# One-core gated mix of linear attention and dilated local attention: resident weight stages, crossbar-transposed x, overlapping key tiles with row-tiled scores, Wo folded into KV

## The chip, the cores and the metric

The kernel runs on one core of a Trainium2 chip. Its time is the device time of one execution in microseconds (us). Engine names are those of the profile: PE is TensorE's matmul, PEld its weight load, DVE is VectorE, ACT is ScalarE, POOL is GpSimd, SP is SyncE, which issues the DMAs.

Ratios are the mean time of one kernel's runs over the mean of the kernel before in the same rounds on the same chip, so they are not quite the ratio of the medians quoted beside them. Where two edited kernels are compared, I take the difference of their ratios times 620 us and say so.

## The reference

The sequence has S = 2048 rows, D = 1024 columns and H = 32 heads of width 32. Both halves read the same `x`.

```python
g = sigmoid((x * gate_w).sum(-1))
# A: linear attention, H = 32 heads of width 32
q, k, v = heads(x @ A_wqkv);  pq, pk = phi(q), phi(k)     # phi(t) = max(t,0) + min(exp(t),1) + 1e-6
kv = einsum("sd,se->de", pk, v);  z = pk.sum(s)           # per head
a = ((pq @ kv) / (pq @ z + 1e-6)) @ A_wo
# B: each query sees 8 keys: its own row, 2, 4, ... 14 rows earlier
q, k, v = heads(x @ B_wqkv)
b = (softmax(q . k[s - 2w], w = 0..7) @ v) @ B_wo
out = g * a + (1 - g) * b                                  # [1, 2048, 1024], bf16
```

## The kernel before

It works in four blocks of 512 rows. Each block loads its rows of `x`, computes the gate from them, transposes them on TensorE, projects, and does B's attention for 8 groups of four heads (a "head group" is 128 columns). A's queries and B's results go to DRAM. When KV is complete, an output phase reads them back, one tile of 128 rows after another.

```python
for t in range(4):                                   # per block: load, gate, transpose
    eng.dma_start(out=xtile[:], in_=x[tb * 128:(tb + 1) * 128, :])
    nc.vector.tensor_tensor_reduce(out=gjunk[:], in0=xtile[:], in1=gw_row[:], ..., accum_out=gdot[:])
    ...
    for kt in range(KT):
        nc.tensor.transpose(out=xps[:, kt, :], in_=xtile[:, kt * 128:(kt + 1) * 128], identity=ident[:])
    # evacuated into xT by VectorE or ScalarE
...
for c in range(KT):                                  # B: per head group; k, q and A's q are projected (cut)
    for i in range(4):                               # queries masked to one head each
        nc.vector.tensor_scalar(out=qm[:, :, i, :], in0=uq_v, scalar1=headmask4[:, i:i + 1], ...)
    for t in range(4):                               # 128 queries against this and the previous 128 keys
        nc.tensor.matmul(s2[:, 0, :], lhsT=kT512[:, c, qcols], rhs=qm_flat, start=True, stop=True)
        nc.tensor.matmul(s2[:, 1, :], lhsT=prev_keys, rhs=qm_flat, start=True, stop=True)
        # exp (ScalarE), mask (VectorE), then per head two PV matmuls of 33 columns, reciprocal, scale, transpose
    nc.sync.dma_start(out=OBT_d[b4, :, c, :], in_=OBTpiece[:])
...
# output phase, per 128 rows: numA and denA from KVbd and Zbd, scale to OA, 8 transposes to OAT,
# then 32 matmuls with the two Wo, copied out and stored
```

The softmax here doesn't subtract the row's maximum and nothing guards it: scores larger than these inputs give would overflow.

## Time and profile before

The time is 620.0 us (median of 4 runs, 619.11 to 620.95).

| What | before |
|---|---|
| PE busy / share of the span | 581.7 us / 94% |
| DVE busy | 355.9 us (58%) |
| ACT busy | 278.9 us (45%) |
| PE's share of the chain that ended last | 84% |
| PE issue time summed from the timeline (estimate) | 557 us of a span of 618.1 us |

Three parts of the page: the first line of busy times, and two rows of the 40 slices (tenths of each slice busy, and the clock granted to TensorE in tenths).

```profile
PE 581.7 (94%) x3980; PEld 284.8 (46%) x4056; DVE 355.9 (58%) x1165; ACT 278.9 (45%) x489; POOL 5.3 (1%) x22
...
PE   3999999979999998999999989999997999999997
...
PEclk9999999999999999999999989999999899999999
```

PE is almost always busy, so a change has to take work away from PE, or close its few gaps. A matmul's recorded duration (about 380 ns for 512 columns) overlaps its neighbour's; the pace has to be read from the chain or the timeline. The first line below is from the chain (start, length, what), the others from PE's timeline of one head group.

```profile
32.53 10.74 PE pj L187 x49
```

```profile
201.07 0.18 PE L301 MATMUL oB<-Vaug,PT 128*128 128x33 bf16 x1
201.10 0.18 PE L303 MATMUL oB<-Vaug,PT 128*128 128x33 bf16 x1
201.12 0.18 PE L301 MATMUL oB<-Vaug,PT 128*128 128x33 bf16 x1
```

A 512-column matmul costs about 0.215 us of issue (the 10.74 us hold 49 of them and the rest of the last one's duration), and a 33-column one 0.025 us, whatever its recorded 0.18 us says. With these paces 2048 projection and output matmuls take 440 us, 248 score matmuls 53 us, 992 PV matmuls 25 us, 384 transposes 21 us, the rest 17 us. The other 60 us are gaps. The view of windows shows the largest: the start, the joints between blocks, and the joint to the output phase. PE is idle for 26 us in these five rows; the rest lies elsewhere or is covered by recorded durations and was not located (columns: length, then busy time and count of each engine, then clock, DMA share and GB/s).

```profile
0.00:14.20 14.20, 3.67 (x32) 3.44 (x33) 9.77 (x48) 3.00 (x6) 5.29 (x22) 1.00 0.86 298
122.00:145.00 23.00, 19.32 (x133) 9.76 (x135) 19.33 (x61) 11.15 (x20) 0.00 (x0) 1.00 0.30 87
236.00:264.00 28.00, 24.04 (x175) 12.06 (x175) 23.57 (x75) 13.07 (x23) 0.00 (x0) 1.00 0.18 53
353.00:380.00 27.00, 24.13 (x160) 11.82 (x162) 18.73 (x55) 11.67 (x18) 0.00 (x0) 0.94 0.05 16
466.00:487.00 21.00, 16.01 (x152) 9.20 (x153) 16.30 (x56) 9.58 (x19) 0.00 (x0) 0.84 0.49 114
```

### The profile page before, as it was taken

To read this page: it belongs to the slowest core of one execution; us is meant where nothing else is said; L and a number is where in the kernel's file an instruction comes from. 1 tells how busy PE (TensorE), PEld (TensorE's weight loads), DVE (VectorE), ACT (ScalarE), POOL (GpSimd) and SP (SyncE) were. 2 spreads that over 40 slices of the span, in tenths; PEclk is the share of its full clock that TensorE was granted. 3 is DMA by queue.
4 is the path that set the end of the run, shared out by engine and by line. 5 is a ranking of instruction groups with operands and counts; after the bars stand their busy time and mean duration, and the time that the engine had idled before them with its cause. 6 is when DMAs were issued, how large, how long until landed. Compare 5 with 4: busy or idle time off the path is not lost.

```text
span 618.1 us, 10399 instructions
## 1 busy us (share of the span) xinstructions
PE 581.7 (94%) x3980; PEld 284.8 (46%) x4056; DVE 355.9 (58%) x1165; ACT 278.9 (45%) x489; POOL 5.3 (1%) x22
## 2 busy tenths in 40 slices
PE   3999999979999998999999989999997999999997
PEld 2445444444444444345444444454443555445443
DVE  6523788892048889801788873058888533444441
ACT  2333666643347666333666643346666122122111
POOL 3000000000000000000000000000000000000000
PEclk9999999999999999999999989999999899999999
DMA  8970001040001003000000100062013333444311
GB/s 305 398 265 1 27 26 35 32 122 2 0 10 35 27 27 103 10 0 1 27 27 27 35 28 0 1 223 81 30 36 101 83 79 89 103 103 103 85 52 35
DMA packets 57666, 42.88 MB, mean 69 GB/s; under 512 B 35984, under 2 KB 48272, under 8 KB 57616
## 3 DMA queue, kind: packets, MB, share of 16 engines
q1 hardware_dynamic: 57616, 42.22, 21.7%
q8 instruction: 31, 0.51, 0.3%
q14 instruction: 19, 0.16, 0.1%
HBM read 29.62 MB, written 12.58 MB: 68 GB/s over the span
## 4 chain that ended last, share of the span: by engine, by line
PE 84%; DVE 7%; ACT 3%; DMA 2%; issue 2%; SPq 0%; ACTq 0%
PE pj L187 22%; PE po L373 18%; PE pjk L240 9%; PE pjq L245 9%; PE pja L257 8%; DVE pk L195 2%; PE oB L303 2%; PE oB L301 2%; PE tr L316 2%; PE numA L349 1%; DMA xtile<-in_A_x_dram 1%; PE kvp L218 1%; ACT e L192 1%; DVE e L193 1%; DVE qm L252 1%
## 5 line engine op out<-in xcount | busy, mean ns | idle before, releaser
L187 PE MATMUL pj<-WAkv,xT 128*128 128x512 bf16 x500 | 116.7, 385 | 7.6 <-DVE pk L195 3.4
L187 PEld LDWEIGHTS <-xT 128*128 128x128 bf16 x768 | 74.9, 98 | 99.4 <-issue 15.1
L240 PE MATMUL pjk<-xT,WBqk 128*128 128x512 bf16 x251 | 73.7, 379 | 0.6
L257 PE MATMUL pja<-xT,WAq 128*128 128x512 bf16 x246 | 63.3, 378 | 0.6
L245 PE MATMUL pjq<-xT,WBqk 128*128 128x512 bf16 x245 | 62.9, 378 | 0.7
L373 PE MATMUL po<-Wo_sb,OAT 128*128 128x512 bf16 x241 | 61.9, 382 | 1.1
L373 PE MATMUL po<-Wo_sb,obtblk 128*128 128x512 bf16 x239 | 61.2, 379 | 0.1
L220 DVE TENSOR_TENSOR KVacc<-KVacc,kvp 128x129 f32<-128x129 f32 x32 | 8.3, 289 | 87.2 <-PE kvp L218 87.2
L187 PE MATMUL pj<-WBv,xT 128*128 128x512 bf16 x250 | 55.4, 379 | 0.3
L252 DVE TENSOR_SCALAR qm<-uq,headmask_118 128x512 bf16<-128x512 bf16 x128 | 42.1, 346 | 15.7 <-ACT uq L248 15.7
L378 DVE CAST osb<-po 128x512 bf16<-128x512 f32 x16 | 11.1, 692 | 54.9 <-ACT osb L376 54.9
L301 PE MATMUL oB<-Vaug,PT 128*128 128x33 bf16 x480 | 40.2, 179 | 0.0
L303 PE MATMUL oB<-Vaug,PT 128*128 128x33 bf16 x480 | 39.5, 178 | 0.0
L313 DVE TENSOR_TENSOR Obc<-oB,scb 128x128 bf16<-128x128 f32 x128 | 36.7, 287 | 1.5
L301 PEld LDWEIGHTS <-PT 128*128 128x128 bf16 x480 | 33.0, 97 | 9.4 <-DVE PT L293 7.7
L260 ACT ACTIVATE ea<-pja 128x512 f32<-128x512 f32 x32 | 19.1, 597 | 37.6 <-PE pja L257 37.4
L198 ACT CAST vA<-pj 128x512 bf16<-128x512 f32 x32 | 18.8, 588 | 37.6 <-PE pj L187 37.6
L192 ACT ACTIVATE e<-pj 128x512 f32<-128x512 f32 x32 | 19.1, 597 | 36.2 <-PE pj L187 32.6
L309 DVE RECIPROCAL scb<-oB 128x4 f32<-128x4 f32 x128 | 23.0, 179 | 21.4 <-PE oB L303 20.6
L240 PEld LDWEIGHTS <-WBqk 128*128 128x128 bf16 x256 | 24.4, 97 | 23.5
L202 ACT CAST Vaug<-pj 128x512 bf16<-128x512 f32 x32 | 18.8, 588 | 36.0 <-PE pj L187 33.8
L245 PEld LDWEIGHTS <-WBqk 128*128 128x128 bf16 x256 | 22.8, 97 | 23.7
(825 smaller groups left out, 901.9 us busy)
## 6 DMA issues: line engine op xcount, KB each, us to landing
xtile<-in_A_x_dram SPq DMA_DIRECT2D x16, 256.0 KB, 4.5
WAkv<-in_A_wqkv_dram SPq DMA_DIRECT2D x16, 256.0 KB, 5.4
WBqk<-in_B_wqkv_dram SPq DMA_DIRECT2D x8, 512.0 KB, 8.1
pqT_d<-pqpiece SPq DMA_DIRECT2D x32, 128.0 KB, 1.9
OBT_d<-OBTpiece SPq DMA_DIRECT2D x32, 128.0 KB, 1.9
out_dram<-osb SPq DMA_DIRECT2D x32, 128.0 KB, 2.6
pqblk<-pqT_d SPq DMA_DIRECT2D x15, 256.0 KB, 3.5
obtblk<-OBT_d SPq DMA_DIRECT2D x15, 256.0 KB, 3.1
```

The lines of the kernel that those rows point to most:

```text
L187: nc.tensor.matmul(pj[:], lhsT=xT[:, kt, xcols], rhs=Wsrc[:, kt, col0:col0 + 512], start=(kt == 0), stop=(kt == KT - 1))
L192: nc.scalar.activation(out=e[:], in_=pj[:], func=ACT.Exp)
L240: nc.tensor.matmul(pjk[:], lhsT=WBqk[:, kt, wcols_k], rhs=xT[:, kt, :], start=(kt == 0), stop=(kt == KT - 1))
L245: nc.tensor.matmul(pjq[:], lhsT=WBqk[:, kt, wcols_q], rhs=xT[:, kt, :], start=(kt == 0), stop=(kt == KT - 1))
L252: nc.vector.tensor_scalar(out=qm[:, :, i, :], in0=uq_v, scalar1=headmask4[:, i:i + 1], scalar2=None, op0=ALU.mult)
L257: nc.tensor.matmul(pja[:], lhsT=WAq[:, kt, wcols_q], rhs=xT[:, kt, :], start=(kt == 0), stop=(kt == KT - 1))
L260: nc.scalar.activation(out=ea[:], in_=pja[:], func=ACT.Exp)
L301: nc.tensor.matmul(oB[:, i, :], lhsT=PT[:, 1, i, :], rhs=Vaug_prev[:, h, :], start=True, stop=False)
L303: nc.tensor.matmul(oB[:, i, :], lhsT=PT[:, 0, i, :], rhs=Vaug_cur[:, h, :], start=False, stop=True)
L309: nc.vector.reciprocal(out=scb[:], in_=oB[:, :, Dh:Dh + 1])
L313: nc.vector.tensor_tensor(out=Obc[:], in0=oB[:, :, 0:Dh], in1=scb[:].broadcast_to([P, 4, Dh]), op=ALU.mult)
L373: nc.tensor.matmul(po[:, nch, :], lhsT=lhsT, rhs=Wo_sb[:, c16, nch * 512:(nch + 1) * 512], start=(c16 == 0), stop=(c16 == 2 * KT - 1))
```

## The change

The intent is to reorganise the kernel into three stages over all 2048 rows, with everything resident on the chip:

1. All of `x` is loaded transposed by the DMA crossbar. A's keys and values, then KV. A's `Wo` is folded into KV (`W2 = KV @ Wo` per head group), so that A's output needs one matmul in place of numerator, transpose and output; the scaling moves to the queries.
2. B: 18 query tiles of 113 rows (the first has 127), each against its own 128 keys that overlap the neighbour's by 15, so that one key tile suffices. Values are projected for each of the 18 tiles. Scores use 32-row tiles of the array, the four heads of a group in four row groups.
3. A's queries, denominators by a matmul with a block of ones times z, `1/den` as exp(-ln(den)), then both outputs; the gate is applied at evacuation.

The new code, cut to its core:

```diff
+    nc.sync.dma_start_transpose(out=xT[:, :, 0:128], in_=x[0:128, :])
+    WkA = load_w("WkA", A_wqkv, D)
+    for s0, s1_ in ((128, 512), (512, 1024), (1024, S)):
+        nc.sync.dma_start_transpose(out=xT[:, :, s0:s1_], in_=x[s0:s1_, :])
...
-                xps = ps_pj.tile([P, KT, P], BF16, name="xps", tag="pj")
-                for kt in range(KT):
-                    nc.tensor.transpose(out=xps[:, kt, :], in_=xtile[:, kt * 128:(kt + 1) * 128],
-                                        identity=ident[:])
...
+            trk = ps_kv.tile([P, P], BF16, name="trk", tag="kv")
+            nc.tensor.transpose(out=trk[:], in_=kvm[:], identity=ident[:])
+            nc.scalar.copy(out=KVT[:, c, :], in_=trk[:])
...
+                nc.tensor.matmul(w2p[:], lhsT=KVT[:, c, :], rhs=WoA[half][:, c, :],
+                                 start=True, stop=True)
...
+                for q0, w, k0 in tiles:                  # three tiles per group
+                    for i in range(4):
+                        r = slice(32 * i, 32 * i + 32)
+                        nc.tensor.matmul(s4[:, i, o:o + w], lhsT=kT[r, k0:k0 + P], rhs=qT[r, q0:q0 + w],
+                                         start=True, stop=True)
+                    o += w
...
+                den = ps_d.tile([P, 512], F32, name="den", tag="den")
+                nc.tensor.matmul(den[:], lhsT=Zb[:, c, :], rhs=pq[:], start=True, stop=True)
+                ld = work.tile([P, 512], F32, name="ld", tag="e", bufs=3)
+                nc.scalar.activation(out=ld[:], in_=den[:], func=ACT.Ln, bias=eps[:])
+                nc.scalar.activation(out=ld[:], in_=ld[:], func=ACT.Exp, scale=-1.0)
+                nc.vector.tensor_tensor(out=pqs[:, c, :], in0=pq[:], in1=ld[:], op=ALU.mult)
...
+                    nc.scalar.activation(out=ob[:], in_=pb[:], func=ACT.Copy, scale=omgall[:, tb:tb + 1])
...
+                    nc.vector.scalar_tensor_tensor(out=osb[:, ncols], in0=pa[:], scalar=gall[:, tb:tb + 1],
+                                                   in1=ob[:], op0=ALU.mult, op1=ALU.add)
```

A scheduler orders the instructions of each engine, so the order on an engine is not the order of this text.

## The prediction

> **What bounds it now.** TensorE. The page has PE busy 94% of 618.1 us, and the chain of waits is 84% PE. In the timeline a 128x512 matmul takes 0.215 us of issue (49 in 10.74 us), a 128x33 probability-times-V matmul 0.025 us, a transpose 0.055 us, a numA/denA pair 0.08 us. Summed: 2048 projection and output matmuls 440 us, 248 scores 53 us, 992 PV 25 us, 384 transposes 21 us, kvp 7 us, numA/denA 10 us: about 557 us. The other 60 us are the start (first projection at 14.2 us, full pace only from 32.5 us), the joints between blocks (PE busy 19.3 of 23 us, 24.0 of 28, 24.1 of 27) where x is gated, transposed and evacuated, the joint to the output phase (16.0 of 21 us), and the tail. VectorE (58%) and ScalarE (45%) are off the path.
>
> **Change, by PE issue time.**
> - Full-width matmuls: 2048 become 2128 (+32 V for overlapping tiles, +32 denominators, +16 folded Wo): +17 us.
> - Scores: 248x512 (53 us) become 576 with 32 rows x 113 columns, four in different row groups. At the 0.025 us pace of the PV matmuls, 12 take 0.3 us, 15 us in all. [...] Scores: about 34 us, saving 19.
> - PV: 992 to 576, -10 us. Transposes 384 to 152, -13 us (x goes by DMA, OA disappears). numA/denA -10 us.
> Sum about 522 us, 35 less.
>
> **Around it.** Start: the first 128 rows of x and 1 MB of weights must land (about 8 us), then 3.75 MB of transposed x queue behind 2 MB of weights on one queue. [...] Start loss about 20 us, like before. The three joints of x (about 11 us of PE idle) disappear; DRAM round trips too, but these were hidden.
> Attention: one scores buffer. Per group: exp 1.3 us (from 1.03 us at 1024 columns), scores 0.3-0.7 us, two handoffs: about 2.1-2.4 us, while PE has about 2.3 us of work per group. ScalarE needs 13 us per head group of four, VectorE 13 us if the mask multiply keeps the 0.69 us/1024 pace, PE about 20. So PE still bounds, with stalls of 0.3-0.5 us per group: 15-20 us. Stage joints (kvp to W2, attention to output) 10 us, tail 5 us.
> 522 + 20 + 17 + 5 minus some overlap: 562 us, range 533 to 597. Faster over 2%: 0.93; within 2%: 0.05; slower: 0.02.
>
> **What would show it.** PE busy stays over 90%; projections keep 0.215 us; the x joints are gone from the slices; the V and output stages run at full pace; an attention period per head group takes 21-24 us; scores wait for exp. Start: first matmul at 7-10 us, then waits for transposed x. ScalarE and VectorE near 60% in attention.
>
> **What would make it wrong.** [...] Odd column offsets (127+113j-15): if they slow weight loads, 576 PV matmuls might go from 0.025 to 0.1 us, +40 us. If row-tiled matmuls don't overlap, [...] +20-30 us. If the mask multiply with rows of 339 and a broadcast operand runs at half pace, VectorE takes 16 us of each period and delays PV. [...]

Passages are cut where marked. Two are parts of the forecast: 0.4 us per group, 19 us in all, for changes between full matmuls and row tiles, which was only the author's guess, and a rate assumed for the transposed loads. The sum: scores 15 + 19 = 34 us (0.3 + 0.4 = 0.7 us per group), which is in the 522 us of issue time; 522 + 20 + 17 + 5 = 564 us, 562 us with the overlap. The 20 us of the start stand on the start of the kernel before (first projection at 14.2 us, full pace from 32.5 us).

## The result

The changed kernel takes 569.25 us (median of 4 runs, 567.71 to 570.23). The ratio to the kernel before is 0.9175 (95% interval 0.9156 to 0.9194): 8.2% faster, 7 us above the predicted 562 us and inside the range. The later repeat gave 570.29 us and a ratio of 0.9192.

The same rows of the page as before:

```profile
PE 530.1 (93%) x3495; PEld 242.9 (43%) x3560; DVE 252.7 (44%) x469; ACT 232.9 (41%) x372; POOL 15.5 (3%) x62
...
PE   2999999996999999999999999969999999999997
...
PEclk9999999999799999999999999988999999999999
```

PE lost 51.6 us of busy time and the span lost 49.6 us. The three joints of `x` are gone from the PE row, and two new dips stand at slices 10 and 27, with a lower clock in slices 11, 27 and 28. The windows view, cut at the stages (same columns as before), gives the ledger:

```profile
0.00:14.10 14.10, 3.57 (x8) 1.09 (x8) 1.87 (x9) 1.88 (x2) 13.54 (x59) 1.00 0.92 236
14.10:125.60 111.50, 110.27 (x495) 49.68 (x506) 52.27 (x97) 36.71 (x63) 1.95 (x4) 1.00 0.55 161
125.60:146.50 20.90, 13.71 (x151) 9.08 (x151) 9.40 (x25) 8.57 (x25) 0.00 (x0) 0.92 0.00 1
146.50:210.50 64.00, 63.50 (x283) 28.74 (x290) 11.79 (x17) 10.58 (x18) 0.00 (x0) 0.97 0.10 33
210.50:224.30 13.80, 13.75 (x68) 6.10 (x68) 2.77 (x4) 2.34 (x4) 0.00 (x0) 1.00 0.24 77
224.30:367.90 143.60, 138.71 (x1559) 67.36 (x1588) 85.17 (x168) 86.12 (x119) 0.00 (x0) 1.00 0.03 9
367.90:383.40 15.50, 10.41 (x175) 5.87 (x177) 10.92 (x22) 10.29 (x13) 0.00 (x0) 0.85 0.01 2
383.40:568.50 185.10, 176.15 (x771) 75.03 (x787) 78.53 (x128) 76.42 (x128) 0.00 (x0) 0.99 0.07 23
```

The eight rows are: the start; A's keys and values; KV and the fold; B's values; the projections of the first head group; seven periods of attention with the next group's projections beside them; the last head group; the output stage. Against the issue time of what each holds (estimates from the 0.215, 0.055 and 0.025 us above):

| Stage | took | issue time of its matmuls | difference |
|---|---|---|---|
| start, A's keys and values | 125.6 us | 110.0 us (512 matmuls) | 15.6 us |
| KV and fold | 20.9 us | 11.0 us | 9.9 us |
| B's values, first projections | 77.8 us | 75.6 us (352) | 2.2 us |
| seven attention periods | 143.6 us | 131 us | 13 us |
| last head group | 15.5 us | 8.5 us | 7.0 us |
| output stage, with its tail | 185.1 us | 168.6 us (784) | 16.5 us |

Issue time is down from an estimated 557 us to 505 us, that is 52 us; the gaps went from about 61 to about 64 us in all. So the change bought what it took away from PE, and replaced the old gaps with new ones of the same size. The timeline of PE shows the row-tiled scores at work:

```profile
304.55 1.89 PE L230 MATMUL pjkq<-xT,WqB_695 128*128 128x512 bf16 x8
306.37 0.34 PE L243 MATMUL s_3043<-qT,kT 32*128 32x127 bf16 x12
306.64 1.68 PE L230 MATMUL pjkq<-xT,WkB_88 128*128 128x512 bf16 x6
```

The eight matmuls before the scores have 8 x 0.215 = 1.72 us of issue, until 306.27; the scores start at 306.37 and the next projection at 306.64. Twelve scores, with the change from full matmuls to 32-row tiles (a mode change, below) and the change back, cost 0.37 us of PE, where I had allowed 0.7 us. In 24 of the 48 groups the twelve stand together like this; in the others the scheduler puts other matmuls between them.

### The profile page after: what moved, and what is told of

The parts are those of the page before. It is cut to its first block, busy times and chain, and to the rows that moved or that the text cites. A ratio compares the mean times of both kernels' runs of the same rounds, so it can differ in the third digit from the quotient of the medians.

```text
span 568.5 us, 8370 instructions
## 1 busy us (share of the span) xinstructions
PE 530.1 (93%) x3495; PEld 242.9 (43%) x3560; DVE 252.7 (44%) x469; ACT 232.9 (41%) x372; POOL 15.5 (3%) x62
## 4 chain that ended last, share of the span: by engine, by line
PE 68%; DVE 16%; ACT 8%; DMA 3%; issue 3%; SPq 1%; DVEq 0%; ACTq 0%
PE pj L129 14%; PE pjkq L230 14%; PE pjv L210 11%; PE pa L326 8%; PE pb L320 7%; DVE pq L305 3%; ACT ld L310 3%; PE pjq L298 3%; PE oB L257 3%; DVE Ob L265 2%; PE den L308 2%; PE tr L270 2%; ACT PT_1362 L249 2%; DMA xT<-in_A_x_dram 2%; DVE gjunk L153 2%
## 5 line engine op out<-in xcount | busy, mean ns | idle before, releaser
L328 DVE SCALAR_TENSOR_TENSOR osb<-pa,gall,ob 128x512 bf16<-128x512 f32 x32 | 23.7, 750 | 56.7 <-PE pa L326 52.3
L323 ACT ACTIVATE ob<-pb,omgall 128x512 f32<-128x512 f32 x32 | 22.0, 687 | 60.5 <-PE pb L320 52.5
L235 DVE CAST qT<-pjkq 128x512 bf16<-128x512 f32 x32 | 22.0, 688 | 42.4 <-PE pjkq L230 39.6
L129 PE MATMUL pj<-WkA_67,xT 128*128 128x512 bf16 x126 | 30.9, 407 | 10.7 <-DMA WkA_67<-in_A_wqkv_dram 8.0
L320 PEld LDWEIGHTS <-OBT 128*128 128x128 bf16 x256 | 25.2, 98 | 29.7 <-issue 0.8
L310 ACT ACTIVATE ld<-den,eps 128x512 f32<-128x512 f32 x32 | 22.0, 687 | 35.7 <-PE den L308 35.7
L320 PE MATMUL pb<-WoB_1336,OBT 128*128 128x512 bf16 x128 | 34.0, 385 | 0.0
L210 PE MATMUL pjv<-WvB_82,xT 128*128 128x512 bf16 x141 | 32.6, 392 | 1.1 <-DVE W_1311 L187 0.8
L230 PE MATMUL pjkq<-xT,WkB_88 128*128 128x512 bf16 x116 | 32.3, 380 | 0.8 <-issue 0.6
L230 PE MATMUL pjkq<-xT,WqB_695 128*128 128x512 bf16 x124 | 32.6, 379 | 0.3
L230 PE MATMUL pjkq<-xT,WkB_86 128*128 128x512 bf16 x119 | 31.8, 379 | 0.7 <-issue 0.5
L298 PE MATMUL pjq<-xT,WqA_1729 128*128 128x512 bf16 x122 | 31.3, 394 | 1.1 <-DVE qT L235 0.6
L230 PE MATMUL pjkq<-xT,WqB_693 128*128 128x512 bf16 x124 | 31.8, 379 | 0.2
L320 PE MATMUL pb<-WoB_1338,OBT 128*128 128x512 bf16 x120 | 31.8, 379 | 0.2
L210 PE MATMUL pjv<-WvB_84,xT 128*128 128x512 bf16 x141 | 31.1, 379 | 0.2
```

The costliest lines, as they stand in the source:

```text
L129: nc.tensor.matmul(pj[:], lhsT=xT[:, kt, t * P:(t + 1) * P], rhs=W[half][:, kt, :], start=(kt == 0), stop=(kt == KT - 1))
L210: nc.tensor.matmul(pj[:], lhsT=xT[:, kt, k0:k0 + P], rhs=WvB[half][:, kt, :], start=(kt == 0), stop=(kt == KT - 1))
L230: nc.tensor.matmul(pj[:], lhsT=W[c // 4][:, kt, (c % 4) * P:(c % 4 + 1) * P], rhs=xT[:, kt, cols], start=(kt == 0), stop=(kt == KT - 1))
L235: nc.vector.tensor_copy(out=dst[:, cols], in_=pj[:])
L298: nc.tensor.matmul(pj[:], lhsT=WqA[c // 4][:, kt, (c % 4) * P:(c % 4 + 1) * P], rhs=xT[:, kt, cols], start=(kt == 0), stop=(kt == KT - 1))
L310: nc.scalar.activation(out=ld[:], in_=den[:], func=ACT.Ln, bias=eps[:])
```

## The experiments

Eleven kernels ran. All gave a result within the tolerance. Two put one part of the change into the kernel before, two take one part out of the changed kernel, four repair one gap each, one repeats the changed kernel unedited, and two put repairs together.

### One part alone: the crossbar

`x` is transposed by DMA in the kernel before; the gate reads its own copy of the rows.

```diff
+            for s0, s1 in (((0, 128), (128, 512)) if b4 == 0 else ((0, 512),)):
+                eng.dma_start_transpose(out=xT[:, :, s0:s1], in_=x[b4 * 512 + s0:b4 * 512 + s1, :])
-                for kt in range(KT):
-                    nc.tensor.transpose(out=xps[:, kt, :], in_=xtile[:, kt * 128:(kt + 1) * 128], identity=ident[:])
-                # and the evacuations of xps
```

> The kernel before with one part of the change alone: x is transposed by the DMA crossbar on its way in, TensorE transposes of x and their evacuations are gone, and the gate still reads its own copy of x. Theory: the joints of the four blocks (about 4 us of PE idle each for three, and the slow start) come from the chain of x row load, gate, transpose, evacuation; 128 transposes (7 us) and most of 11 us of idle vanish: 14 to 20 us faster than before, about 603. Rival (the joints come from the end of attention, not from x): only the 7 us of transposes, 4 to 8 us faster.

Measured: 603.85 us, ratio 0.974 (0.9725 to 0.9754), 16 us faster than before. The sums of three windows of 14 us that enclose the three joints between blocks, first of the kernel before (at 122, 236 and 353 us) and then of this one (at 113, 225 and 339 us):

```profile
sum 42.00, PE 34.19 PEld 19.23 DVE 38.10 ACT 24.54 POOL 0.00; mean PE 11.39 PEld 6.41 DVE 12.70 ACT 8.18 POOL 0.00
```

```profile
sum 42.00, PE 38.62 PEld 19.13 DVE 35.80 ACT 26.54 POOL 0.00; mean PE 12.87 PEld 6.38 DVE 11.93 ACT 8.85 POOL 0.00
```

PE's idle time in them falls from 7.8 to 3.4 us, and 128 transposes leave PE. So the theory holds, and the rival's 4 to 8 us is excluded: the chain of loading, gating and transposing `x` was a cost beyond its PE time. The two together are an estimated 11.4 us (4.4 and 7.0). A part of the remaining 5 us may be clock (an estimated 1.7 us, 0.12 x 14 us): the third window of the kernel before has a mean granted clock of 0.88, the three of this run 1.00. The rest I have not traced.

### One part alone: row-tiled scores

```diff
-                    s2 = ps_s.tile([P, 2, 512], F32, name="s2", tag="s")        # two buffers
-                    nc.tensor.matmul(s2[:, 0, :], lhsT=kT512[:, c, qcols], rhs=qm_flat, start=True, stop=True)
+                    s2 = ps_s.tile([P, 4, 512], F32, name="s2", tag="s")        # one buffer
+                    for kb in range(nkb):
+                        for i in range(4):      # keys: rows 32i..32i+31 of this or the previous key block
+                            nc.tensor.matmul(s2[:, i, kb * P:(kb + 1) * P], lhsT=keys, rhs=uq[r, qcols], ...)
```

> The kernel before with one part of the change alone: scores in 32-row tiles of the array, four head rows at once, against the same two blocks of 128 keys; no masked queries, [...]. Theory: eight matmuls of 128 columns per block cost about 0.35 us of PE against 0.43 us, 10 us less in all, and VectorE loses 42 us which nobody waits for; with a single scores buffer about half is lost in waits: between 10 us faster and 5 us slower. Rival (row tiling is where the change gets its speed): 20 us or more faster.

Measured: 611.39 us, ratio 0.9866 (0.9849 to 0.9882), 8 us faster. That is under 2%, but the interval excludes no change. It is near the good end of the theory's range and far from the rival's 20 us: row tiling by itself is a small part of the 51 us. VectorE's busy time fell from 355.9 to 326.1 us; how much of the 8 us this gave was not separated.

### One part undone: row tiles

Scores over all 128 rows of a head group, wrong.

```diff
-                        nc.tensor.matmul(s4[:, i, o:o + w], lhsT=kT[r, k0:k0 + P], rhs=qT[r, q0:q0 + w],
+                        nc.tensor.matmul(s4[:, i, o:o + w], lhsT=kT[:, k0:k0 + P], rhs=qT[:, q0:q0 + w],
```

> The changed kernel with its scores computed over all 128 rows of the head group (wrong result on purpose): the same 576 score matmuls of 113 or 127 columns, but none in a 32-row tile, so no row group works beside another and no tiling mode changes. Theory (row groups overlap, mode changes cost about 0.1 us): twelve scores cost 0.64 us instead of 0.37 us of PE; 48 groups, PE bound in seven of eight periods: a period of 20.5 us becomes 21.5-22.2 and the kernel 8 to 14 us slower. Rival 1 (issue bound): matmuls are paced by issue and the row groups gain nothing; no change within 2 us. Rival 2 (my prediction: [...] 0.7 us per group in all): it is as fast or up to 5 us faster.

Measured: 575.65 us, ratio 0.9286 (0.9256 to 0.9315), which is (0.9286 - 0.9175) x 620 = 7 us slower than the changed kernel. PE's timeline at the same place as above:

```profile
308.70 0.79 PE L243 MATMUL s<-qT,kT 128*128 128x127 bf16 x12
309.33 1.67 PE L230 MATMUL pjkq<-xT,WkB 128*128 128x512 bf16 x6
```

Twelve scores now take 0.63 us, as the theory said, against 0.27 us and 0.1 us on entering the row tiles. Both rivals fall: the row groups do work beside one another, and the mode changes do not cost the 0.4 us per group that I had guessed. The period grew from 20.51 to 21.19 us (start of one head group's first scores to the next), 0.68 us, less than 6 x 0.26 us, and seven such periods make 4.8 us. A likely reason is that part went into waits that the faster scores had spent on the exponential, but that was not traced. The difference of two ratios is uncertain by about 2 us, so the miss on size (7 us where 8 to 14 were expected) is small.

Its scores are wrong; the check of this problem does not see an error in B's scores of that kind. Here only its times matter.

### One part undone: the fold

The masked KV multiplies the queries in the output stage; W2, its transposes and its evacuations go.

```diff
-            trk = ps_kv.tile([P, P], BF16, name="trk", tag="kv")      # and W2: 8 transposes, 16 matmuls, 24 evacuations
+                num = ps_n.tile([P, 512], F32, name="num", tag="num")
+                nc.tensor.matmul(num[:], lhsT=KVbd[:, c, :], rhs=pq[:], start=True, stop=True)
-                nc.vector.tensor_tensor(out=pqs[:, c, :], in0=pq[:], in1=ld[:], op=ALU.mult)
+                nc.vector.tensor_tensor(out=pqs[:, c, :], in0=num[:], in1=ld[:], op=ALU.mult)
```

> The changed kernel with the fold of Wo into KV undone: the masked KV multiplies the queries in the output stage (32 matmuls of 512 more), and the 8 transposes, 16 matmuls and their evacuations between the A values and the B values are gone. Theory: the fold saves 3 us of PE issue and costs its joint: that falls from 21 us to 8-9 us, and the added matmuls stand in a chain that has 0.3 us to spare per step; 6 to 13 us faster than the changed kernel. Rival (the fold pays): 3 to 7 us slower.

Measured: 560.68 us, ratio 0.9044 (0.9028 to 0.906): (0.9175 - 0.9044) x 620 = 8 us faster than the changed kernel, although 32 matmuls came and 16 went. The chain at that joint (start, length, what):

```profile
126.22 7.31 PE kvp L165 x128
133.53 0.22 PE pjv L194
```

The joint is 7.3 us in place of 20.9. As built, the fold cost more than it saved. In the output stage the chain of this run shows why the added matmuls did not cost their full 6.9 us: they stand in a loop that PE does not bind.

```profile
419.53 0.39 PE den L292
...
419.94 0.69 ACT ld L296
420.63 0.50 ACT e L285
...
421.15 0.44 DVE e L286
...
421.61 0.70 DVE pq L289
...
422.36 0.40 PE den L292
```

From one denominator matmul to the next it is 2.83 us: the logarithm of head group c, the exponential of c+1 behind it on ScalarE, and two VectorE operations that lead to the denominators of c+1.

### Repair of the output stage: denominators one head group late

```diff
+                if c > 0:
+                    den_step(c - 1, pq_prev)       # den matmul, ln, exp, product of the previous head group
+                pq_prev = pq
+            den_step(KT - 1, pq_prev)
```

> The changed kernel with one edit in the output stage: the denominator matmul, its logarithm and exponential and the product of head group c are emitted after the query projection and the exponential of head group c+1. Theory (order on ScalarE): the logarithm of c waits for the denominators of c, the exponential of c+1 stands behind it on ScalarE, and the denominators of c+1 wait for that exponential, so each step of 8 is a closed chain of 2.91 us where PE has 2.57 us of work. Then the waits of the denominators' weight load on pq (15.1 us in all) vanish, a block of four row tiles falls from 45.6 to 43.0-43.6 us, and the kernel gets 7 to 11 us faster (about 560). Rival (throughput): ScalarE has 1.9 us of work per step and only two PSUM buffers, so the stall only moves; less than 3 us.

The loop in the changed kernel's own chain (pieces of issue time cut):

```profile
434.42 0.39 PE den L308
...
434.84 0.69 ACT ld L310
435.52 0.50 ACT e_4607 L301
436.04 0.44 DVE e_4607 L302
...
436.58 0.70 DVE pq L305
...
437.32 0.40 PE den L308
```

Measured: 562.57 us, ratio 0.9061 (0.9042 to 0.908): (0.9175 - 0.9061) x 620 = 7 us faster than the changed kernel. The edit also gives `pq` a third buffer, since two head groups are now under way at once; the chain above shows no wait for a `pq` buffer. In the chain of the second block the denominators now follow the projections directly:

```profile
431.11 0.22 PE den L297
431.32 1.73 PE pjq L306 x8
433.05 0.32 PE den L297
```

A step takes 2.0 us, a block 44.04 us (425.41 to 469.45) where the changed kernel has 45.6 us (428.0 to 473.6). So the loop was the cause, and the rival (ScalarE's amount of work) falls, since that amount is the same: the step was 2.9 us (434.42 to 437.32) and is 2.0 us. Two details missed: the block did not get to 43.6 us, because after the eighth projection the chain goes through ScalarE from 441.21 to 445.00, with an output evacuation standing between two denominators' logarithms; and the weight load's wait for pq fell from 15.1 to 10.1 us, not to nothing.

### Repair of the joint of KV and fold

The transpose of head group c is issued after the KV product of c+1 and has its own PSUM buffers; the ones of V are set by GpSimd.

```diff
+        ps_tr = s1.enter_context(tc.tile_pool(name="ps_tr", bufs=2, space=bass.MemoryType.PSUM))
+            if c > 0:
+                fold(c - 1, kvms[c - 1])           # transpose and copy
+            if c > 1:
+                fold2(0, c - 2)                    # first half of W2; the second half follows the loop
-        nc.vector.memset(V[:, :, :, Dh:Dh + 1], 1.0)
+        nc.gpsimd.memset(V[:, :, :, Dh:Dh + 1], 1.0)
```

> The changed kernel with the joint between the A values and the B values reordered: the transpose of KV of head group c is issued after the KV product of c+1 and has PSUM buffers of its own, and the ones of V are set by GpSimd and not by VectorE. Theory (chain): the joint of 21 us (125.6 to 146.5) holds 11 us of PE issue; 8 waits of about 0.7 us for the masked KV and one of 2.6 us behind the memset of V make the rest, and they bring the half clock of 6.8 us after it. The joint falls to 13-15 us, the half clock disappears or shrinks; 6 to 9 us faster. Rival (evacuation bound): sixteen evacuations of the folded Wo and eight of KV bind the joint, less than 3 us.

Measured: 561.84 us, ratio 0.9049 (0.9035 to 0.9063): 8 us faster than the changed kernel, by the same sum. The joint is 14.4 us (126.16 to 140.58) and the trace has no half clock there. The chain of waits was the cause, since the evacuations of the rival are as many as before; how much each part of the edit gave (order, PSUM buffers, memset) was not separated. The longest of these waits, in PE's timeline of the changed kernel:

```profile
141.69 0.23 PE L174 MATMUL trk<-ident,kvm 128*128 128x128 bf16 x1 [2.58 <-DVE kvm L170]
```

One part of the repair worked badly, as the timeline of the repaired kernel shows:

```profile
134.17 0.28 DVE L192 TENSOR_SCALAR Zb<-bdmask,zc 128x128 bf16<-128x128 f32 x1
135.00 2.61 POOL L221 MEMSET V<- 128x576 bf16 x1 [118.90 <-ACT W L178]
135.36 2.33 DVE L192 TENSOR_SCALAR Zb<-bdmask,zc 128x128 bf16<-128x128 f32 x1
```

The same VectorE operation that takes 0.28 us took 2.33 us and ended with GpSimd's memset; the chain passes through it. That GpSimd's memset (135.00 to 137.61 us) held up the VectorE operation (135.36 to 137.69 us) is my reading of these times; the trace does not show how, and no run here tries the memset elsewhere.

### Repair of the start: order of loads

```diff
-    WkA = load_w("WkA", A_wqkv, D)
-    for s0, s1_ in ((128, 512), (512, 1024), (1024, S)):
+    WkA = load_w("WkA", A_wqkv, D, mid=lambda: nc.sync.dma_start_transpose(out=xT[:, :, 128:512], in_=x[128:512, :]))
+    for s0, s1_ in ((512, 1024), (1024, S)):
```

> The changed kernel with one edit in the order of loads: rows 128 to 512 of transposed x are asked for before the second half of the first weights. Theory (queueing): the second row tile waits from 11.5 to 14.1 us because its transpose is queued behind 1 MB of weights which nobody needs before 41 us; it then lands at 10-11 us, PE does not stop after the first tile, and 3 to 4 us are saved. Rival (slow transposes): the 0.75 MB transpose needs its 10.7 us from issue to landing whatever stands before it; then less than 1.5 us, within noise.

Measured: 567.2 us, ratio 0.9139 (0.9108 to 0.9169). That is 2 us less than the changed kernel and the intervals overlap, so the time alone is inconclusive. The traces show more: the first KV product starts at 123.75 us here, and at 125.56 to 126.65 us in the profiles of the changed kernel, its repeat and the three other repairs, which all have the old start. PE's timeline of the changed kernel and of this one:

```profile
7.95 3.57 PE L129 MATMUL pj<-WkA_67,xT 128*128 128x512 bf16 x8 [7.95 <-DMA WkA_67<-in_A_wqkv_dram]
14.13 27.40 PE L129 MATMUL pj<-WkA_67,xT 128*128 128x512 bf16 x118 [2.60 <-DMA xT<-in_A_x_dram]
```

```profile
8.10 9.23 PE L131 MATMUL pj<-WkA,xT 128*128 128x512 bf16 x32 [8.10 <-DMA WkA<-in_A_wqkv_dram]
18.42 3.84 PE L131 MATMUL pj<-WkA,xT 128*128 128x512 bf16 x17 [1.09 <-DMA xT<-in_A_x_dram]
```

The wait for the second row tile is gone, so the load queued before that transpose was the cause of this wait: the transpose was issued 0.6 us sooner and landed 8.6 us later, not 10.7 us. Those 8.6 us remain, so the transpose's own speed is not cleared altogether. New waits of 1.1 and 0.8 us stand at the next transposes, which fits a gain below the expected 3 to 4 us, and the half clock at the KV joint happened to last 10.2 us in this profile against 6.8 us in the other.

### Repair of the last head group

A's first query block gets buffers that are free during attention, and its denominators come after all eight projections. To make room, the row of gate weights moves to a pool of the first stage and B's `Wo` is loaded after attention (not in this cut).

```diff
+    e0p = ctx.enter_context(tc.tile_pool(name="e0p", bufs=2))                 # exists during stage 2
+        pqs0 = wpool.tile([P, KT, 512], BF16, name="pqs0", tag="w")           # a weight buffer
+                pq = pqs[:, c, :]                                             # scaled in place later
+            for c in range(KT) if b == 0 else []:
+                den_step(c, pqs[:, c, :])
```

> The changed kernel with the first block of A's queries made able to run beside the last head group of attention: its exponential has a buffer of its own from the start of the second stage, pq is written straight into its final tile in a weight buffer, and the denominators of this block come after all eight projections. Theory (buffers): from 367.9 us on only 16 of 64 projections can be issued before the scores' buffers are released, PE is idle about 6 us and falls to half clock for 10 us. Now some 37 projections fill the last head group; the half clock at 379-389 us is gone, and 9 to 14 us are saved. Rival (evacuation): ScalarE and VectorE, which have the exponentials, masks and now eight pq as well, bind this stretch; less than 4 us.

Measured: 558.52 us, ratio 0.9002 (0.8984 to 0.902): 11 us faster than the changed kernel. The half clock at that joint is gone from the trace. The last head group with the projections beside it (same columns as the other windows) is:

```profile
366.90:382.90 16.00, 15.00 (x207) 7.77 (x207) 13.79 (x30) 12.67 (x18) 0.00 (x0) 1.00 0.01 2
```

PE is busy for 15.0 of 16.0 us, where it was 10.4 of 15.5 us. The projections could not run before because the output stage's buffers for the exponential and for pq lay in memory that stage 2 still held: with these, the order and the two loads changed, the projections fill the gap. The rival falls, since PE stays busy although VectorE and ScalarE have more to do.

This was the second build of this repair. A first one, with the denominators moved but the exponential's buffer still allocated in the output stage, left the order of instructions in the last head group as it was (still 16 of 64 projections) and was not run.

### Everything together

> The changed kernel itself, unedited, on the same chip and in the same rounds as the next two, as their yardstick: 567 to 571 us, ratio to the kernel before 0.915 to 0.920.

> The changed kernel with the four repairs together: order of loads at the start, KV transposes one head group late with their own PSUM buffers and the ones of V set by GpSimd, A's first query block beside the last head group of attention, denominators one head group late. Theory (the four are separate stretches of PE idle time; only the last two share the first output block): the gains of 2.2, 7.8, 10.7 and 7.1 us add up but for 2 to 4 us: 543 to 546 us. Rival (what is freed is lost again in the next stretch): above 552 us.

> The same repairs at the start, the last head group and the denominators, but with the fold of Wo into KV undone in place of its repair. Theory: the joint falls from 14.4 us (repaired fold) to 7.4 us, and 32 matmuls of 0.215 us come in the output stage, where no slack is left now: equal to the repaired fold within 3 us, 542 to 548 us. Rival (unfolded is better because the fold's gain is nothing): 4 us or more faster than the repaired fold.

| Kernel (5 rounds, same chip) | median | ratio to before |
|---|---|---|
| changed kernel again | 570.29 us | 0.9192 (0.9169 to 0.9215) |
| four repairs (4 runs) | 546.62 us | 0.8812 (0.8798 to 0.8826) |
| three repairs, fold undone | 544.0 us | 0.8774 (0.8762 to 0.8786) |

The four repairs gain (0.9192 - 0.8812) x 620 = 24 us where the single gains add up to 28; the theory allowed 2 to 4 us less, for the two that share the first output block; that these are the reason was not traced. The median lies 0.6 us above the upper end of 543 to 546 us. Without the fold it is 2 us better still: within the 3 us that the theory allowed, but the intervals do not touch, so the unfolded kernel is the fastest here. The page of that run:

```profile
PE 524.0 (97%) x3568; PEld 243.4 (45%) x3568; DVE 249.6 (46%) x461; ACT 228.1 (42%) x356; POOL 15.7 (3%) x62
...
PE   4899999999999999999999999999999999999997
...
PEclk9999999999999999999999999999999999999999
```

The dips at the two joints are gone, and with them the half clock: the mean granted clock is 1.000, against 0.985 in the changed kernel's profile.

## Why the prediction was right

The sum came out 7 us low, 562 for 569 us, and that it came so near is partly luck. Issue time was 17 us less than forecast (505 for 522 us), and the gaps were 22 us more (64 us for the 42 us in the sum: 20 for the start, 17 for attention, 5 for the tail). The 10 us for stage joints are named in the prediction but missing from its sum, and the output stage was taken to have no gaps.

- **Bound by PE, and work taken from PE is time.** Right. The predicted drop of issue time was 35 us; with the scores' real cost it was 52 us, and the time fell by 51 us. The two single parts that were tried in the kernel before (16 and 8 us) make half of it. The other half was not tried alone and is only summed from paces: one key tile where there were two (an estimated 22 us: 124 scores groups of 0.32 us in the row-tiled run against 48 of 0.37 us), fewer PV matmuls (10 us), no numA and denA and no transposes of OA (17 us), less 17 us for added matmuls: 32 us in sum, before the new gaps.
- **Scores at 0.7 us per group.** Mis-sized: 0.37 us, shown in the timeline and by the run with 128 rows. Over 48 groups this is an estimated 16 us of PE that I counted and that was not there. Of the 0.7 us, 0.4 us were my guess for the mode changes, which no trace had shown; entering the row tiles cost 0.1 us.
- **Attention.** Nearly right. A period took 20.5 us (143.6 / 7), just below the predicted 21 to 24 us, VectorE and ScalarE were busy for 59 and 60% of these periods (predicted near 60%), and the stalls were about 13 us over seven periods, below the predicted 15 to 20 us.
- **Start.** Right in kind: the first matmul at 7.95 us, then a wait for transposed x, and a loss of 15.6 us against "about 20". About 3 us of it (estimate) is pace: the first 14 matmuls start 0.43 us apart, the later ones 0.216 us, although the clock in that row reads 1.00. The crossbar was not slow enough to hurt: PE never waited for it after 14.13 us, and from 0 to 14.1 us all loads, transposes among them, moved at 236 GB/s. No run times the transposes alone, so their own rate is not shown.
- **Stage joints, 10 us.** Mis-sized. The KV and fold joint alone lost 9.9 us plus half clock after it; the last head group lost 7 us and half clock after it. The runs that repair these two gained 8 and 11 us.
- **"The output stage runs at full pace".** Wrong, and the one step with a wrong mechanism: the prediction looks at how busy ScalarE and VectorE are and has no sum for this stage's chain of waits. The steps of 2.9 us come from a loop through the order of ScalarE's queue, which an engine's busy share does not show. The run that changes the order (and gives pq a third buffer) gained 7 us with the same work.
- **The dangers I named** did not come: odd column offsets left PV at 0.025 us (12 in 0.30 to 0.32 us in 36 of 48 groups) and its weight loads at a median of 96 to 97 ns (96 ns before), and the mask multiply of 1412 columns took 0.90 us, no slower than the pace of 0.69 us for 1024.

## What to carry to other kernels

Count issue time, not recorded busy time (here 0.215 us against 0.38 us for a 512-column matmul), to see what a change takes from a bound engine; but look for the new gaps at every place where a pool ends or a stage begins: here buffers that reused the old stage's memory kept the next stage's work from filling the hole (11 us, with the order and two loads changed too). Where a step's chain stands behind the next step's work in one engine's queue, emit it one step late: that gained 7 us here. A fold that saves a few matmuls can be worth less than nothing if it stands alone in a serial joint: here it cost 8 us as first built, and 2 us after its repair.

## What the traces showed of the clock, the row tiles and the transposes

- The KV joint, with eight gaps of 0.36 to 0.62 us and one of 2.58 us between short bursts (PE busy 13.7 of 20.9 us), was followed by half clock from 143.1 us for 6.8 us. Whether one of these gaps goes with the half clock, and which, was not tested apart. The view of windows over that stretch:

```profile
143.10:149.90 6.80, 5.70 (x13) 1.73 (x13) 2.96 (x5) 2.06 (x4) 0.00 (x0) 0.50 0.45 150
```

- The effect varies by run: the same unedited KV joint had half clock for 6.8, 3.4, 10.2, 3.4 and 10.2 us in five profiles (changed kernel, late denominators, order of loads, last head group, changed kernel again; mean granted clock over the whole span 0.985, 0.985, 0.982, 0.994 and 0.979), and the last head group 10.2 us in the first three and the last of these. Some microseconds between two runs of a kernel with such a joint go with this: of the nine runs of the changed kernel the shortest, 567.71 us, had a mean clock of 0.991 and the longest, 572.11 us, 0.979.
- The mode change took about 0.1 us on entering the row-tiled scores (306.27 to 306.37 us), and no extra time on leaving was seen (the next projection followed the twelve scores after 0.27 us).
- Four row tiles of 113 to 127 columns beside one another were 1.7 times as fast as full-height scores (0.63 to 0.37 us for twelve scores), the mode change included.
- In the changed kernel the first crossbar transpose, of 128 rows, held SP, which issues it, for 1.34 us and the next three for 20.33 us together; weights behind them are issued that much later. An ordinary 1 MB weight load held SP for 0.56 us before these three, and 0.58 to 4.41 us after them, so how much of the 20.33 us is the transposes' own and how much a full queue is not shown.
